# Block-local attention and two expert layers: how the first layer's weights are re-joined and split again, and when later weights are converted

## The chip, the cores and the metric

The kernel runs on one core of one Trainium2 chip. The metric is the device time of one execution in microseconds (us). Engines are named as in the profile: PE is TensorE (matrix products; PEld its weight loads), DVE is VectorE, ACT is ScalarE, POOL is GpSimd and SP is SyncE, which here only issues transfers. ACT also issues some transfers.

## The reference, cut to what matters

Everything is float32 in the inputs (the weights arrive as 64-bit floats, which the kernel converts from their integer halves).

```python
# attention: 4 x 8 heads, 768 positions of 64, in chunks of 32 with a short context
scores = scale * np.matmul(q_c, k_full.transpose(0, 1, 3, 2))
a = np.exp(scores - np.max(scores, axis=-1, keepdims=True))
out = np.matmul(a / (np.sum(a, axis=-1, keepdims=True) + 1e-09), v_full)
x = out.transpose(0, 2, 1, 3).reshape(3072, 512)
# first layer, 512 -> 1536 -> 512
x = (1.0 / (1.0 + np.exp(-(x @ w_gate))) * (x @ w_val)) @ w_out
# second layer, 512 -> 1024 -> 512
h = x @ w_in
solu = h * softmax(h)
ln = (solu - mean) / np.sqrt(var + 1e-06) * g_ln
return ln @ w_out2
```

## The kernel before, in words

**Blocks and stages.** The 3072 tokens are 24 tiles of 128, in 6 blocks of 512 (`j` from 0 to 5). Attention makes one tile of x at a time. For each block the up projection (`up`, line 694) goes over 12 chunks `m` of 128 hidden units, each for the gate and for the value: `up(j, m, gv)` is 12 matmuls of 128x512. Its result goes through a sigmoid (ACT, line 700) and a product (DVE, line 707 or 709) and is stored to DRAM. Only when all six blocks are up does the down projection start (line 801), followed by the second layer. TensorE runs the six blocks' up steps one after another, with the attention of later tiles between them.

**Two forms of the first layer's weights.** All products keep nearly float32 exactness by writing each operand as a high part plus a low part and adding three products. For blocks 0 and 1 the parts of a weight chunk are two 32-bit tiles, `wa[m]` (line 285 high, on ACT; line 236 low, on POOL). For blocks 2 to 5 they are two 16-bit tiles, `wh[m]`, which take the place of `wa[m]` in memory once `up(1, m, 1)` has read it. The re-making goes in steps:

- `r_max` (line 300): the absolute maximum of each of the 24 high parts, on DVE; `r_top` takes the largest per partition, and `hop` spreads it over the partitions (below).
- `r_set` (line 305): from the maxima a power of two as scale, in three small DVE instructions.
- `r_sum(m)` (line 308): high plus low back into one float32 tile `w32[m % 2]`, on POOL (recorded at line 312). There are two such tiles, so chunk m+2 waits for the low part of chunk m.
- `r_hi(m, gv)`: `w32` times the scale, rounded to 16 bits, on ACT (recorded at line 482).
- `r_lo(m, gv)`: `w32` times the scale minus the high part, on DVE (recorded at line 238, tile `wh`).

**A maximum over partitions.** `across` (line 461) does it on DVE alone: a 32x32 block transpose, a maximum, three copies of one element to the first partition (line 466), a maximum of four, four copies of one row of 32 equal elements back to partitions 0, 32, 64, 96 (line 469), another transpose. It is used 14 times.

**Later weights.** The weights of the three later products (28 pieces of 128x512) are loaded as 64-bit floats, converted (ACT line 220; DVE lines 225, 226, 229), scaled and split like the others and stored to DRAM (lines 401, 404). Before that, eight pieces of the last weight are loaded once more for their maxima alone (`p_load`, `p_max`), and block 0's twelve products are read back for theirs (`g_again`, `g_max0`). All these use a ring of three buffers `r`.

**The order.** A planner (`Plan`, line 18) orders all work by hand-given durations, dependencies, buffers and due times; the program text of each engine is its result, and each engine runs its queue strictly in that order. A task may start at most `AHEAD` = 40 us before its due time in the planner's own clock. Due times run back from the up steps, which are due one after another:

```python
FIRST, RATE, LEAD, SLACK, EARLY, LATER = 30.0, 1.12, 30.0, 3.0, 140.0, 235.0
one("wst", n, SP, 0.1, c_store, ..., due=LATER + 11.0 * (n - NU))          # later weights, n - NU from 0 to 27
one("rmax", n, DVE, 0.69, ..., ["whi"], due=FIRST + 70 + 2.5 * n)
one("pmax", i, DVE, 0.75, p_max, ["pld"], ..., due=EARLY + 8.0 * i)
add(("gmax", 0, m), DVE, 0.75, ..., due=EARLY + 4 + 8.0 * m)
```

`SHIFTS` adds small random shifts to the due times given by hand, from fixed seeds. Attention's loads of q, k and v, the stores of products, the transposes of x (line 672) and the reloads of block 0's products are issued on SP's queue; the later weights' loads and the eight loads for maxima on ACT's.

Of the kernel before, what the change touches and what calls it, by code (L numbers as in the profile page):

```python
# [9 lines left out]
F32 = mybir.dt.float32  # L10
# [11 lines left out]
class Plan:  # L22
# [7 lines left out]

    SHIFTS = [(2019, 0.3), (2226, 0.3), (6910, 1), (6082, 0.3), (4955, 0.3), (915, 0.3), (2444, 0.3)]

# [100 lines left out]
def encoder_kernel(  # L133
# [15 lines left out]
    nc = tc.nc  # L149
# [19 lines left out]
    const = ctx.enter_context(tc.tile_pool(name="const", bufs=1))  # L169
    turn = const.tile([128, 2, 32], F32, name="turn")  # L170
    tiny = const.tile([128, 4 * MF + 4 * K2 + 7 * NB + 22], F32, name="tiny")
# [119 lines left out]

    wh = {}

    def pow2_scale(s, p, m):
# [4 lines left out]
    def r_max(m, gv):  # L299
        absmax(WM[:, m, gv:gv + 1], wa[m][:, gv, 0].bitcast(F32))  # L300

    def r_top(gv):
        nc.vector.tensor_reduce(out=PG[:, gv:gv + 1], in_=WM[:, :, gv], axis=AX.X, op=ALU.max)

    def r_set():
        pow2_scale(SG, PG, PG)

# [10 lines left out]

    def r_lo(m, gv):
        lo_part(wh[m][:, gv, 1], W["f32"][:, m % 2, gv], wh[m][:, gv, 0], SG[:, gv:gv + 1])  # L320

# [5 lines left out]
    def absmax(dst, a):  # L327
        nc.vector.tensor_reduce(out=dst, in_=a, axis=AX.X, op=ALU.max, apply_absolute_value=True)  # L328
# [132 lines left out]
    def across(a):  # L461
        nc.vector.tensor_copy(turn[:, 0, 0:1], a)
        nc.vector.transpose(turn[:, 1], turn[:, 0])
        nc.vector.tensor_reduce(out=turn[:, 0, 1:2], in_=turn[:, 1], axis=AX.X, op=ALU.max)
        for x in range(1, 4):
            nc.vector.tensor_copy(turn[0:1, 0, 1 + x:2 + x], turn[32 * x:32 * x + 1, 0, 1:2])
        nc.vector.tensor_reduce(out=turn[0:1, 0, 5:6], in_=turn[0:1, 0, 1:5], axis=AX.X, op=ALU.max)
        for x in range(4):
            nc.vector.tensor_copy(turn[32 * x:32 * x + 1, 1], turn[0:1, 0, 5:6].to_broadcast([1, 32]))
        nc.vector.transpose(turn[:, 0], turn[:, 1])  # L470
        nc.vector.tensor_copy(a, turn[:, 0, 0:1])

    def hop(name, a, deps):
        add(name, DVE, 1.0, lambda: across(a), deps=deps + ["turn"])

# [489 lines left out]
    ACT, DVE, POOL, PE, SP = "act", "dve", "pool", "pe", "sp"  # L965
    FIRST, RATE, LEAD, SLACK, EARLY, LATER = 30.0, 1.12, 30.0, 3.0, 140.0, 235.0

# [22 lines left out]
    for t in range(NTILE):  # L990
# [23 lines left out]
        if t >= 4 * J16:  # L1014
            j = t // 4
            if t % 4 == 0:
# [5 lines left out]
                add(("isc", j), DVE, 0.2, lambda j=j: scales(j), deps=[("vset", j), "rset"])  # L1022
            one("xhi", t, ACT, 0.71, x_hi, ["norm", ("vset", j)], acq=[("w", ("xs", t))])
            one("xlo", t, DVE, 0.75, x_lo, ["xhi"], rel=[("s", t)])
            for y in range(2):
# [13 lines left out]
    for n, (m, gv, _) in enumerate(pieces):  # L1039
# [5 lines left out]
        if n >= NU:  # L1045
# [11 lines left out]
            if keep:  # L1057
                one("wlo", n, DVE, 0.76, c_lo, ["whi"], rel=[("w", n)])
            one("wst", n, SP, 0.1, c_store, ["wlo" if keep else ("w2imax", w2_piece.index(n))], rel=[key if keep else ("w", n)], dma=[0.73],
                due=LATER + 11.0 * (n - NU))  # L1060
            continue
# [3 lines left out]
        one("wlo", n, POOL, 1.4, w_lo, ["whi"], rel=[("w", n)])  # L1065
        one("rmax", n, DVE, 0.69, lambda n: r_max(*divmod(n, 2)), ["whi"], due=FIRST + 70 + 2.5 * n)
        if gv == 0:
            continue
        one("rsum", m, POOL, 2.5, r_sum, [("wlo", n - 1), ("wlo", n)] + [("rlo", m - 2, y) for y in range(2) if m > 1]
            + [("dx", 4 * J16 - 4)] * (m == 0),  # L1070
            acq=[("x", "w32")] if m == 0 else [])
        for z in range(2):
            add(("rhi", m, z), ACT, 0.72, lambda m=m, z=z: r_hi(m, z), deps=["rset", ("rsum", m), ("up", J16 - 1, m, 1, (0, 512))] + [("rhi", m, 0)] * z)
            add(("rlo", m, z), DVE, 0.76, lambda m=m, z=z: r_lo(m, z), deps=[("rhi", m, z)],
                rel=[("x", "w32")] if (m, z) == (MF - 1, 1) else [])
    for f in range(MF):
# [26 lines left out]
    for y in range(2):  # L1103
        add(("rtop", y), DVE, 0.1, lambda y=y: r_top(y), deps=[("rmax", 2 * m + y) for m in range(MF)])
        hop(("rspr", y), PG[:, y:y + 1], [("rtop", y)])
    add("rset", DVE, 0.3, r_set, deps=[("rspr", 0), ("rspr", 1)])
    clock = FIRST
    for j in range(NB):
        steps = steps_of(j)
        seen = set()  # L1110
        for s, (m, w) in enumerate(steps):
# [6 lines left out]
            for gv in range(2):  # L1118
                clock += (2.73 if j < J16 else 2.6) * RATE
                deps = [("up", j, m, 0, w)]  # L1120
                if gv == 0:
                    deps = [("wlo", 2 * m + x) if j < J16 else ("rlo", m, x) for x in range(2)] + [
                        ("xlo", 4 * j + x) if j < J16 else ("xtr", 4 * j + x, 1) for x in range(w[0] // 128, w[1] // 128)
                    ]
                elif s == len(steps) - 1:
                    deps += [("up", j, y, 1, z) for y, z in steps[:-1]]
                add(("up", j, m, gv, w), PE, 2.73 if j < J16 else 2.6, lambda j=j, m=m, gv=gv, w=w: up(j, m, gv, w),
                    deps=deps, acq=[] if gv else [("u0", key), ("u1", key)], due=clock,
                    rel=[("x", (y, j)) for y in "hl"[:2 if j < J16 else 1]] if gv and s == len(steps) - 1 else [])
# [154 lines left out]
```

## Time and profile before

| what | value |
|---|---|
| runs | 951.31 us median of 3 (949.44 to 952.26) |
| the profiled execution | 952.16 us, of which 950.4 us from the first to the last instruction (the span) |
| mean granted TensorE clock over the span | 0.983 |
| busy share of the span | PE 95%, PEld 51%, DVE 71%, ACT 51%, POOL 12% |
| blocks 0 to 5 start on TensorE at | 43.0, 136.2, 220.5, 307.1, 384.9, 461.3 us; the last up step ends at 523.6 |

A busy share is an average over stages with different limits. TensorE's matmuls are pipelined and their ends are modelled, so their busy time says that TensorE had work, not that it ran at its peak. The clock is given as a share of full speed (2.4 GHz). A row of a timeline carries in brackets how long its engine had been idle before it and what ended the wait; where that engine runs its queue in order, the wait's cause can lie further back.

### The profile page before, as it was taken

Reading aid. Unit: us, or ns where it says so; the run is one execution under the profiler, and the core shown is the slowest. Engines: PE = TensorE matmul, PEld = TensorE weight load, DVE = VectorE, ACT = ScalarE, POOL = GpSimd, SP = SyncE. Lnnn points to the kernel's source line nnn. Section 1 sums busy time; section 2 is a strip of 40 time slices with the busy share of each in tenths; the row PEclk is TensorE's granted clock in tenths of the full one; section 3 lists DMA queues with packets and bytes.
Section 4 is the critical chain, followed back from the end, with each engine's and each line's share of the span. In section 5 each row is a group of like instructions: output and inputs, shape, how many; then the busy total and the mean of one; then the engine's idle time right before and its main releaser. Section 6 shows DMA issues by size and latency. Waiting matters only on the chain.

```text
span 950.4 us, 18091 instructions
## 1 busy us (share of the span) xinstructions
PE 902.0 (95%) x7080; PEld 487.2 (51%) x7080; DVE 677.1 (71%) x1333; ACT 481.2 (51%) x810; POOL 117.6 (12%) x150
## 2 busy tenths in 40 slices
PE   5698998997899899999999999999999999999998
PEld 4486787774554454444444444444444444444443
DVE  3788999979874875788729556884874963867581
ACT  4467632733762692575546345553643633645452
POOL 1153330323200000000005200000000000000000
PEclk9699999999999999999999999999999999999999
DMA  9999946593797679655772622444154244242333
GB/s 171 272 215 242 219 114 179 135 215 98 188 197 164 205 164 194 195 146 145 257 272 100 213 89 75 92 100 99 56 119 97 73 101 100 67 100 45 78 67 99
DMA packets 219157, 136.85 MB, mean 144 GB/s; under 512 B 170176, under 2 KB 184512, under 8 KB 219072
## 3 DMA queue, kind: packets, MB, share of 16 engines
q1 hardware_dynamic: 208832, 109.48, 48.9%
q10 hardware_dynamic: 10240, 26.22, 9.1%
q8 instruction: 55, 0.90, 0.4%
q14 instruction: 30, 0.25, 0.1%
HBM read 86.38 MB, written 33.03 MB: 126 GB/s over the span
## 4 chain that ended last, share of the span: by engine, by line
PE 70%; DVE 15%; DMA 7%; issue 3%; ACT 2%; SPq 2%; POOL 0%; ACTq 0%; DVEq 0%; POOLq 0%
PE u L694 22%; PE y L801 19%; PE ps L944 13%; PE Q L854 5%; PE R L854 3%; PE P L854 3%; PE tr L496 3%; DVE tiny L328 2%; PE ps L555 2%; DVE w L226 2%; DMA r<-in_moe_w_in_dram 2%; DVE wh L238 1%; DVE w L225 1%; DVE g L709 1%; DMA mm<-in_mem_k_dram 1%
## 5 line engine op out<-in xcount | busy, mean ns | idle before, releaser
L694 PE MATMUL u<-x,wh 128*128 128x512 f16 x1152 | 255.4, 380 | 2.9 <-DMA x<-w 1.9
L694 PEld LDWEIGHTS <-wh 128*128 128x128 f16 x1152 | 112.1, 98 | 134.3 <-issue 5.6
L801 PE MATMUL y<-gh,pl 128*128 128x512 f16 x576 | 176.5, 379 | 1.1 <-ACT gh L482 1.1
L801 PEld LDWEIGHTS <-pl 128*128 128x128 f16 x864 | 84.5, 98 | 104.5 <-issue 2.9
L694 PE MATMUL u<-xh,wa 128*128 128x512 f32 x384 | 127.6, 404 | 3.8 <-DVE g L707 2.2
L944 PE MATMUL ps<-wo,nt 128*128 128x512 f16 x576 | 127.6, 379 | 0.8 <-ACT o L951 0.8
L482 ACT ACTIVATE gh<-gi,gm 128x512 f16<-128x512 f32 x72 | 51.3, 719 | 122.8 <-PE y L801 117.6
L801 PE MATMUL y<-gl,pl 128*128 128x512 f16 x288 | 109.1, 379 | 0.9 <-DVE gl L238 0.9
L238 DVE SCALAR_TENSOR_TENSOR gl<-gi,gm,gh 128x512 f16<-128x512 f32 x72 | 53.5, 749 | 62.6 <-ACT gh L482 62.4
L944 PEld LDWEIGHTS <-nt 128*128 128x128 f16 x576 | 56.3, 98 | 69.0 <-issue 1.1
L694 PEld LDWEIGHTS u<-xh,wa 128*128 128x128 f32 x384 | 73.8, 192 | 21.5 <-DVE g L707 3.3
L694 PE MATMUL u<-xl,wa 128*128 128x512 f32 x192 | 76.4, 398 | 0.4 <-DVE xl L680 0.4
L716 ACT ACTIVATE sg<-g,tiny 128x512 f32<-128x512 f32 x48 | 34.7, 722 | 55.6 <-DVE g L709 51.4
L709 DVE SCALAR_TENSOR_TENSOR g<-u,tiny,sg 128x512 f32<-128x512 f32 x48 | 35.8, 747 | 35.0 <-PE u L694 27.1
L854 PEld LDWEIGHTS <-yh 128*128 128x128 f16 x336 | 32.9, 98 | 39.6
L913 POOL TENSOR_TENSOR ls<-ls,tiny 128x1 f32<-128x1 f32 x24 | 14.8, 617 | 301.5 <-DVE ls L909 294.7
L220 ACT ACTIVATE w<-r 128x512 f32<-128x512 f32 x46 | 31.1, 676 | 35.6 <-DMA r<-in_moe_w_gate_dram 10.2
L875 DVE TENSOR_TENSOR pl<-Q,pl 128x512 f32<-128x512 f32 x36 | 24.7, 687 | 29.5 <-PE Q L854 29.4
L854 PE MATMUL Q<-pl,yh 128*128 128x512 f16 x144 | 42.8, 379 | 0.0
L700 ACT ACTIVATE sg<-u,tiny 128x512 f32<-128x512 f32 x48 | 32.8, 682 | 18.8 <-PE u L694 15.0
L694 PEld LDWEIGHTS u<-xl,wa 128*128 128x128 f32 x192 | 37.0, 193 | 8.1 <-DVE xl L680 0.9
L236 POOL TENSOR_TENSOR wa<-w,wa 128x512 fp32r<-128x512 f32 x24 | 33.2, 1386 | 60.0 <-ACT wa L285 60.0
(144 smaller groups left out, 1355.2 us busy)
## 6 DMA issues: line engine op xcount, KB each, us to landing
gd<-g SPq DMA_DIRECT2D x72, 256.0 KB
gi<-gd SPq DMA_DIRECT2D x72, 256.0 KB
r<-in_moe_w_out_dram ACTq DMA_DIRECT2D x28, 512.0 KB
vw<-in_v_dram SPq DMA_DIRECT2D x64, 98.0 KB
rk<-in_k_dram SPq DMA_DIRECT2D x24, 256.0 KB
rq<-in_q_dram SPq DMA_DIRECT2D x24, 256.0 KB
out_dram<-o SPq DMA_DIRECT2D x24, 256.0 KB
wd<-r SPq DMA_DIRECT2D x20, 256.0 KB
```

Source lines behind the costliest of these rows:

```text
L220: nc.scalar.activation(out=dst, in_=raw[:, :, 1].bitcast(F32), func=AF.Copy, scale=2.0 ** -112)
L236: nc.gpsimd.tensor_tensor(out=dst, in0=x, in1=hi, op=ALU.subtract)
L238: nc.vector.scalar_tensor_tensor(out=dst, in0=x, scalar=s, in1=hi, op0=ALU.mult, op1=ALU.subtract)
L482: nc.scalar.activation(out=dst, in_=x, func=AF.Copy, scale=s)
L496: nc.tensor.transpose(pv[:, kk, :], src[:, 2 * kk:2 * kk + 2, :], ident[0:rows, 0:rows])
L694: nc.tensor.matmul(u, lhsT=a, rhs=c[:, kk, w[0]:w[1]], start=(n == 0), stop=(n == 3 * KM - 1))
L700: nc.scalar.activation(out=sg, in_=U.pop((j, m, 0, w)), func=AF.Sigmoid, scale=1.0 if j < J16 else IS[:, j, 0:1])
L709: nc.vector.scalar_tensor_tensor(out=g, in0=u, scalar=IS[:, j, 1:2], in1=sg, op0=ALU.mult, op1=ALU.mult)
L716: nc.scalar.activation(out=rest, in_=g, func=AF.Square, scale=CS[:, j:j + 1], accum_out=GM[:, j, m:m + 1])
L801: nc.tensor.matmul(y, lhsT=a, rhs=c, start=(f == 0 and n == 0), stop=(f == MF - 1 and n == 2))
L854: nc.tensor.matmul(ps, lhsT=yc[a][:, c, kk, u * 128:(u + 1) * 128], rhs=t[:, hl, kk, :], start=(first and n == 0), stop=(n == 5), skip_gro ...
L944: nc.tensor.matmul(ps, lhsT=nt[:, a, kk, :], rhs=C["wo2"][:, c, kk, :], start=(n == 0), stop=(n == 3 * K2 - 1))
```

## The change

- The weight maxima become sums of squares on ACT, with the accumulator read that the product maxima of blocks 2 to 5 already use; two POOL powers (`r_root`) turn the largest sum into a scale.
- The joined weight `w32` is scaled by ACT in place (`r_scale`), which no longer waits for block 1's last use of the chunk; one ACT instruction per chunk rounds both halves to 16 bits (`r_hi2`), one POOL instruction subtracts for the low part (`r_lo2`).
- `across` copies one element to three partitions and fills the rows with one addition over 128x32.
- The maxima of the last weight and of block 0's products are due 95 us later; the later weights' stores are due from 275 us in steps of 10 instead of from 235 in steps of 11. A few planner durations and the seeds are new, and the x parts of tiles 8 and later wait for the last first-pass low part.

```diff
-    SHIFTS = [(2019, 0.3), (2226, 0.3), (6910, 1), (6082, 0.3), (4955, 0.3), (915, 0.3), (2444, 0.3)]
+    SHIFTS = [(203, 0.5), (476, 0.5), (6692, 0.3), (7115, 3), (2438, 0.3), (525, 0.5), (5342, 0.3)]
...
+    junk = stg[0].tile([128, 512], BF16, name="junk", bufs=1)
...
     def r_max(m, gv):
-        absmax(WM[:, m, gv:gv + 1], wa[m][:, gv, 0].bitcast(F32))
+        nc.scalar.activation(out=junk, in_=wa[m][:, gv, 0].bitcast(F32), func=AF.Square, scale=2.0 ** -16, accum_out=WM[:, m, gv:gv + 1])
 
     def r_top(gv):
-        nc.vector.tensor_reduce(out=PG[:, gv:gv + 1], in_=WM[:, :, gv], axis=AX.X, op=ALU.max)
+        a = PG[:, gv:gv + 1]
+        nc.vector.tensor_reduce(out=a, in_=WM[:, :, gv], axis=AX.X, op=ALU.max)
+        nc.vector.tensor_single_scalar(out=a, in_=a, scalar=2.0 ** -100, op=ALU.max)
+
+    def r_root():
+        for y in range(2):
+            nc.gpsimd.tensor_tensor(out=SG[:, y:y + 1], in0=PG[:, y:y + 1], in1=mhalf, op=ALU.pow)
 
     def r_set():
-        pow2_scale(SG, PG, PG)
+        nc.vector.tensor_single_scalar(out=SG, in_=SG, scalar=2.0 ** -2, op=ALU.mult)
+        pow2(SG)
+        nc.vector.reciprocal(out=PG, in_=SG)
...
-    def r_lo(m, gv):
-        lo_part(wh[m][:, gv, 1], W["f32"][:, m % 2, gv], wh[m][:, gv, 0], SG[:, gv:gv + 1])
+    def r_scale(m, gv):
+        hi_part(W["f32"][:, m % 2, gv], W["f32"][:, m % 2, gv], SG[:, gv:gv + 1])
+
+    def r_hi2(m):
+        wh[m] = wpool.tile([128, 2, 2, 512], F16, tag=f"wa{m}", name=f"wh{m}")
+        nc.scalar.copy(wh[m][:, :, 0], W["f32"][:, m % 2])
+
+    def r_lo2(m):
+        nc.gpsimd.tensor_tensor(out=wh[m][:, :, 1], in0=W["f32"][:, m % 2], in1=wh[m][:, :, 0], op=ALU.subtract)
...
-        for x in range(4):
-            nc.vector.tensor_copy(turn[32 * x:32 * x + 1, 1], turn[0:1, 0, 5:6].to_broadcast([1, 32]))
+        for x in range(1, 4):
+            nc.vector.tensor_copy(turn[32 * x:32 * x + 1, 0, 5:6], turn[0:1, 0, 5:6])
+        nc.vector.tensor_scalar(out=turn[:, 1], in0=turn[:, 2], scalar1=turn[:, 0, 5:6], scalar2=None, op0=ALU.add)
...
-        add(name, DVE, 1.0, lambda: across(a), deps=deps + ["turn"])
+        add(name, DVE, 2.0, lambda: across(a), deps=deps + ["turn"])
...
-    FIRST, RATE, LEAD, SLACK, EARLY, LATER = 30.0, 1.12, 30.0, 3.0, 140.0, 235.0
+    FIRST, RATE, LEAD, SLACK, EARLY, LATER = 30.0, 1.12, 30.0, 3.0, 235.0, 275.0
...
-            one("xhi", t, ACT, 0.71, x_hi, ["norm", ("vset", j)], acq=[("w", ("xs", t))])
-            one("xlo", t, DVE, 0.75, x_lo, ["xhi"], rel=[("s", t)])
+            one("xhi", t, ACT, 0.71, x_hi, ["norm", ("vset", j)] + [("wlo", 2 * MF - 1)] * (t > 7), acq=[("w", ("xs", t))])
+            one("xlo", t, DVE, 0.9, x_lo, ["xhi"], rel=[("s", t)])
...
-                due=LATER + 11.0 * (n - NU))
+                due=LATER + 10.0 * (n - NU))
...
-        one("rmax", n, DVE, 0.69, lambda n: r_max(*divmod(n, 2)), ["whi"], due=FIRST + 70 + 2.5 * n)
+        one("rmax", n, ACT, 0.95, lambda n: r_max(*divmod(n, 2)), ["whi"], due=FIRST + 90 + 2.5 * n)
...
         for z in range(2):
-            add(("rhi", m, z), ACT, 0.72, lambda m=m, z=z: r_hi(m, z), deps=["rset", ("rsum", m), ("up", J16 - 1, m, 1, (0, 512))] + [("rhi", m, 0)] * z)
-            add(("rlo", m, z), DVE, 0.76, lambda m=m, z=z: r_lo(m, z), deps=[("rhi", m, z)],
-                rel=[("x", "w32")] if (m, z) == (MF - 1, 1) else [])
+            add(("rsc", m, z), ACT, 0.72, lambda m=m, z=z: r_scale(m, z), deps=["rset", ("rsum", m)] + [("rsc", m, 0)] * z)
+        add(("rhi", m), ACT, 1.04, lambda m=m: r_hi2(m), deps=[("rsc", m, 1), ("up", J16 - 1, m, 1, (0, 512))])
+        add(("rlo", m), POOL, 2.45, lambda m=m: r_lo2(m), deps=[("rhi", m)], rel=[("x", "w32")] if m == MF - 1 else [])
...
-    add("rset", DVE, 0.3, r_set, deps=[("rspr", 0), ("rspr", 1)])
+    add("rroot", POOL, 1.3, r_root, deps=[("rspr", 0), ("rspr", 1), "mhalf"])
+    add("rset", DVE, 0.45, r_set, deps=["rroot"])
```

## Rows read from the trace of the kernel before

**Rows 1.** TensorE's blocks 0, 1, 2, 5: busy by engine (count), clock, DMA share, GB/s

```profile
43.00:136.20 93.20, 87.61 (x941) 70.45 (x942) 83.46 (x136) 56.56 (x104) 36.40 (x41) 0.96 0.94 215
136.20:220.50 84.30, 79.41 (x774) 62.82 (x773) 76.59 (x138) 36.39 (x59) 23.17 (x15) 0.98 0.71 167
220.50:307.10 86.60, 78.11 (x856) 40.06 (x857) 62.69 (x138) 44.68 (x89) 12.52 (x21) 0.98 0.69 153
...
461.30:523.60 62.30, 62.30 (x290) 28.24 (x289) 38.69 (x59) 33.81 (x54) 14.39 (x6) 1.00 0.59 205
```

**Rows 2.** timeline of TensorE, long waits of 156 to 238 us (start, length, [idle before])

```profile
156.14 0.66 PE L496 MATMUL tr<-ident,s 128*128 128x128 f32 x4 [2.39 <-ACT qT L544]
...
206.02 0.50 PE L694 MATMUL u<-xh,wa 128*128 128x512 f32 x1 [1.46 <-DVE g L707]
...
222.78 7.71 PE L694 MATMUL u<-x,wh 128*128 128x512 f16 x35 [1.94 <-DMA x<-w]
...
231.97 0.66 PE L496 MATMUL tr<-ident,rk 128*128 128x128 f32 x4 [1.48 <-ACT sg L700]
...
237.79 0.66 PE L496 MATMUL tr<-ident,rq 128*128 128x128 f32 x4 [2.58 <-DVE g L709]
```

**Rows 3.** timelines of ScalarE and GpSimd, what stood before those waits

```profile
155.50 0.59 ACT L544 COPY qT<-tr 128x512 f32<-128x512 f32 x1 [4.93 <-DVE tiny L328]
...
227.62 2.35 POOL L312 TENSOR_TENSOR w<-wa 128x1024 f32<-128x1024 f32 x1 [8.63 <-DVE tiny L341]
...
230.01 1.33 ACT L482 ACTIVATE wh<-w,tiny 128x512 f16<-128x512 f32 x2 [9.16 <-POOL w L312]
```

**Rows 4.** stretches of 5 us, granted clock behind the engines' busy times

```profile
155.00:160.00 5.00, 3.86 (x13) 3.13 (x14) 4.74 (x18) 2.00 (x6) 0.67 (x4) 0.72 0.84 229
240.00:245.00 5.00, 4.05 (x14) 1.45 (x12) 4.55 (x22) 1.78 (x5) 2.13 (x4) 0.75 0.80 176
```

**Rows 5.** groups of instructions, whole run: busy us, mean ns | idle before

```profile
L716 ACT ACTIVATE sg<-g,tiny 128x512 f32<-128x512 f32 x48 | 34.7, 722 | 55.6 <-DVE g L709 51.4 <-DMA wo<-wd 4.1
...
L312 POOL TENSOR_TENSOR w<-wa 128x1024 f32<-128x1024 f32 x12 | 29.2, 2439 | 68.4 <-DVE wh L238 47.2 <-PE u L694 8.7 <-DVE tiny L341 8.6
...
L238 DVE SCALAR_TENSOR_TENSOR wh<-w,tiny,wh 128x512 f16<-128x512 f32 x24 | 22.0, 943 | 0.0
...
L443 POOL TENSOR_TENSOR pl<-pl,pl 128x1024 f16<-128x1024 f32 x7 | 17.6, 2537 | 104.0 <-ACT pl L440 100.9 <-DVE w L229 3.1
...
L328 DVE TENSOR_REDUCE tiny<-wa 128x1 f32<-128x512 f32 x24 | 15.1, 674 | 0.0
...
L469 DVE COPY turn<-turn 1x32 f32<-1x32 f32 x56 | 14.3, 256 | 1.0
...
L716 ACT ACTIVATION_READ_ACCUMULATOR sg<-g,tiny 128x1 f32 x48 | 9.1, 190 | 0.0
...
L440 ACT CAST pl<-pl 128x1024 f16<-128x1024 f32 x7 | 7.1, 1034 | 0.4 <-PE u L694 0.4
...
L466 DVE COPY turn<-turn 1x1 f32<-1x1 f32 x42 | 6.0, 143 | 0.9
...
L732 POOL TENSOR_TENSOR tiny<-tiny 128x1 f32<-128x1 f32 x4 | 3.5, 864 | 82.1 <-DVE tiny L1163 82.1
```

**Rows 6.** one tile; one line (136 to 164 us): ns min/median/max, first and last start

```profile
L238 DVE SCALAR_TENSOR_TENSOR wh<-w,tiny,wh x24: 740/742/2872, 166.9 to 247.8; 128x512 f16<-128x512 f32 x24
...
L469 DVE COPY turn<-turn x12: 169/172/2339, 136.5 to 162.7; 1x32 f32<-1x32 f32 x12
```

**Rows 7.** chain that ended last: start us, length, instructions

```profile
440.59 67.46 PE u L694 x312
```

**Rows 8.** stretches where the transfers leave and where they go, columns as above

```profile
140.00:180.00 40.00, 37.60 (x411) 29.92 (x410) 38.74 (x91) 17.13 (x27) 6.73 (x7) 0.96 0.59 164
240.00:340.00 100.00, 95.89 (x1133) 50.14 (x1132) 72.55 (x167) 61.24 (x121) 8.30 (x25) 0.99 0.79 190
```

**Rows 9.** groups of VectorE instructions from 260 to 307 us

```profile
L328 DVE TENSOR_REDUCE tiny<-vw 128x1 f32<-128x2048 f32 x2 | 4.6, 2286 | 11.1 <-DMA vw<-mv 11.1
```

More of the change, by code (lines that the diff above doesn't have):

```diff
@@ L169, in encoder_kernel @@
     const = ctx.enter_context(tc.tile_pool(name="const", bufs=1))
-    turn = const.tile([128, 2, 32], F32, name="turn")
+    turn = const.tile([128, 3, 32], F32, name="turn")
     tiny = const.tile([128, 4 * MF + 4 * K2 + 7 * NB + 22], F32, name="tiny")
@@ L1065, in encoder_kernel @@
         one("wlo", n, POOL, 1.4, w_lo, ["whi"], rel=[("w", n)])
-        one("rmax", n, DVE, 0.69, lambda n: r_max(*divmod(n, 2)), ["whi"], due=FIRST + 70 + 2.5 * n)
+        one("rmax", n, ACT, 0.95, lambda n: r_max(*divmod(n, 2)), ["whi"], due=FIRST + 90 + 2.5 * n)
         if gv == 0:
             continue
-        one("rsum", m, POOL, 2.5, r_sum, [("wlo", n - 1), ("wlo", n)] + [("rlo", m - 2, y) for y in range(2) if m > 1]
+        one("rsum", m, POOL, 2.5, r_sum, [("wlo", n - 1), ("wlo", n)] + [("rlo", m - 2)] * (m > 1)
             + [("dx", 4 * J16 - 4)] * (m == 0),
@@ L1121, in encoder_kernel @@
                 if gv == 0:
-                    deps = [("wlo", 2 * m + x) if j < J16 else ("rlo", m, x) for x in range(2)] + [
+                    deps = [("wlo", 2 * m + x) if j < J16 else ("rlo", m) for x in range(2)] + [
                         ("xlo", 4 * j + x) if j < J16 else ("xtr", 4 * j + x, 1) for x in range(w[0] // 128, w[1] // 128)
```

## Prediction, made before the change was run

> **What bounds the kernel now.** I read the stretches first: one call that cuts the span where TensorE starts token block 0, 1, 2 and so on. The reader is to see that TensorE is busy for 79.4 of block 1's 84.3 us and 78.1 of block 2's 86.6 us, so it is idle for 4.9 and 8.5 us, 13.4 together; in block 5 it never waits [rows 1]. VectorE is busy for 76.6 of the 84.3 us of block 1, and 83.5 of 93.2 in block 0 [rows 1]. TensorE is the limit everywhere else; in blocks 1 and 2 it waits for something that VectorE's queue holds back.
>
> Then the timeline of TensorE, for its long waits: 2.39 us at 156, 1.46 at 206, 1.94 at 222.8, 1.48 at 232.0 and 2.58 at 237.8, together 9.85 us [rows 2]. Two name VectorE's product, one a transposed x that VectorE's part precedes, two ScalarE. So I ask what held ScalarE and GpSimd. In their timelines ScalarE idled 4.93 us behind a VectorE maximum before the qT copy at 155.5, and GpSimd 8.63 us behind VectorE's work on the last weight's maxima (line 341) before the weight sum at 227.6; ScalarE's low-precision weights then waited 9.16 us for that sum [rows 3]. All five waits lead back to VectorE.
>
> Last, the granted clock. After the long waits it averages 0.72 over 155 to 160 us and 0.75 over 240 to 245 [rows 4], so it is partly at 1.2 GHz, the lower of its two levels; at 2.4 GHz that time holds 0.28 and 0.25 times 5 us more work, 2.65 us. What blocks 1 and 2 can give back is therefore 13.4 + 2.65 = **16.0 us**.
>
> **The change part by part.**
>
> Weight maxima. 24 VectorE maxima of 0.674 us go, 15.1 us on its engine [rows 5]. ScalarE gets 24 squares with an accumulator read. The squares of the product maxima are that form: 0.722 + 0.190 = 0.912 us [rows 5], 21.9 us in all. ScalarE is busy for 36.4 of 84.3 us in block 1 but 56.6 of 93.2 in block 0 [rows 1], and some squares can go there. Bound on TensorE: from 0 (they fill ScalarE's idle time) to 5.6 us, which would double block 0's idle time of 93.2 - 87.6; I take 1, because the due times (120 us and later in the planner) lie mostly past block 0's crowded first half. The root is two GpSimd powers of 0.864 us [rows 5], 1.7 us more in a chain that ends with the scales near 164; the first low part comes at 166.9 [rows 6], and TensorE wants it only at 220, so this is hidden by block 1 and would show only if the chain were 50 us late.
>
> Joined weights. 24 VectorE low parts go, 22.0 us [rows 5]. ScalarE keeps its 24 scalings and gets 12 conversions of twice the length, 12 x 1.034 = 12.4 us; GpSimd gets 12 subtractions. The nearest GpSimd row is the same form (f16 from f32, 128x1024), 2.537 us, so 30.4 us beside its 12 sums of 2.439 [rows 5]. Per weight chunk GpSimd works 4.98 us. Run wholly in series (sum 2.44, two scalings at the square's 0.72, conversion 1.03, low part 2.54) a chunk takes 7.4 us, and 12 of them 89 us: from 164 to 253. TensorE uses one chunk per 5.19 us (67.46 us for 312 matmuls, 24 a chunk [rows 7]) plus attention, about 7.2 us in block 2 (86.6 / 12), so its last chunk is due near 300. The low parts before took from 166.9 to 247.8 [rows 6]. I take 0 for it; at the ends, -2 us (chunks ready sooner) and +5 (below).
>
> What GpSimd does to VectorE shows in the rows: a low part has a median of 0.742 us but a longest of 2.872, and a row copy a median of 0.172 but a longest of 2.339 [rows 6], about one GpSimd sum more. The means of all, 0.943 and 0.256 [rows 5], put the loss at 24 x 0.20 + 56 x 0.084 = 9.5 us over 12 sums, 0.8 us per long GpSimd instruction. Twelve more cost VectorE about 9.5 us by this.
>
> The Trainium skill, GPSIMD Engine Reference, Key points, says that GpSimd shares its SBUF interfaces with VectorE, which contends in instructions with two SBUF inputs or in a two-port mode, and that VectorE is about twice as fast at elementwise work. The trace agrees with both (2.54 us against two of 0.742), and by that rule alone this part would be a loss. What it would do here is rival (b).
>
> Row copies. 56 copies of 0.256 us become 42 copies of one element at 0.143 and 14 additions over 128x32, which I put at 0.256 for want of a row: 14.3 - 6.0 - 3.6 = 4.7 us less on VectorE [rows 5]. Only the chain before the scales and the block maxima see it; beyond VectorE's relief I take 0 (ends 0 and -2).
>
> Later conversions. Eight loads and maxima of w2_out and twelve reloads and maxima of block 0's products are due 95 us later, 20 x 0.674 = 13.5 us of VectorE out of block 1 (the shape of the weight maxima [rows 5]); the conversions start 40 us later and end 13 us later (275 + 270 against 235 + 297). What moves is 8 x 512 KB on ScalarE's DMA queue and 12 x 256 KB on SP's, 7.34 MB. Where they leave, the DMA engines are 0.59 busy; where they go (240 to 340) 0.79 at 190 GB/s [rows 8]. At 190 / 0.79 = 240 GB/s they need 31 us, against 21 us free; the conversions that leave this stretch (40 us at one piece of 0.77 MB per 11 us, 2.8 MB) give back 12. It just fits: I take 1 us, ends 0 and 18 (below). At the other end VectorE is busy for 38.7 of block 5's 62.3 us [rows 1], which covers one or two more pieces; if not, they meet the start of the down projection, 0 to 4 us; I take 1.
>
> The planner's durations, its new random shifts and the x order reorder every queue slightly: 0, ends -4 and +4. That later x parts wait for the last first-pass low part costs nothing: GpSimd had done it long before the first of them.
>
> **Sum.** VectorE loses 15.1 + 13.5 + 22.0 + 4.7 = 55.3 us and is held 9.5 longer: some 46 us of relief, nearly all of it in blocks 1 and 2. It is then no longer the last to arrive, and the five waits (9.85 us) and the clock loss (2.65) go, 12.5 us; what remains of the 16.0 I leave standing. New costs 1 + 1 + 1 = 3. Net -9.5 on the profiled execution's 952.16 us gives 942.7; that execution was 0.85 above the median of the runs, so **942 us**.
>
> **Rivals.**
> (a) *Latency instead of VectorE.* The waits pass to the attention chain (ScalarE's copies, loads, transposes), and only 2 us or less is gained: about 950. For it: VectorE itself waited 11.1 us for v loads in block 2 [rows 9], so loads are the next to be late. Against it: all five waits lead back to VectorE. 0.10.
> (b) *GpSimd eats the relief.* VectorE is held by each of 24 long GpSimd instructions for a whole 2.5 us, not 0.8, 60 us, more than the 55 that the change takes from it; block 2's share of the gain, about 6 us with its clock, is lost: near 948. Against: the maxima, which have one input, are not stretched (mean 0.674 [rows 5]), and the row copies and low parts, which are, leave VectorE. 0.10.
> (c) *Slower: the moved loads starve block 3.* The 20 transfers lie ahead of block 3's v loads. In the 60 us before block 3 starts at 307, only 0.21 x 60 = 12.6 us of the DMA engines is free, so v comes 31 - 12.6 = 18 us late, and TensorE, in order, has nothing else: 942 + 18 = 960. SP's queue adds to it, since a reload that waits for one of three buffers holds the attention loads behind it. It decides from 9.5 us of delay on. Against: the pieces moved out, and due times that put attention first. 0.10.
> (d) The change does what it says (the forms are in the code); I give no chance to the opposite.
>
> **How the numbers follow.** Forecast 0.70, (a) 0.10, (b) 0.10, (c) 0.10. A measurement of this kernel can tell about 0.3%, 2.9 us, from no change: 948.5 to 954.2. The forecast's own range is 931 to 948: 16 us and 4 of reordering at one end, half the gain eaten by the upper bounds at the other. With (a) and most of (b) the range is 931 to 953; (c) is left out, and a little of the forecast's tail. Faster: 0.70 and half of (b), 0.75; same: (a) and most of the rest of (b), 0.14; slower: (c) and a remnant, 0.11.
>
> **What would show it.** Right: TensorE's idle time in blocks 1 and 2 falls from 13.4 us to about 4; VectorE's share of block 1 falls from 0.91 to about 0.6; the clock stays at 1.00 from 150 to 245; the low parts on GpSimd end before 255; the row copies have no 2 us outlier. Wrong: TensorE waiting for x from a transpose, or for v, at the start of block 2 or 3 with DMA above 0.9 (c); TensorE waiting for GpSimd's low parts, or VectorE's instructions stretched beside them (b); or waits as long as before under new names (a).

## The result and the profile after

| | before | after | predicted |
|---|---|---|---|
| median of the runs on one chip | 950.60 us (949.44 to 952.26) | **935.49 us** (933.94 to 937.92) | 942 (931 to 953) |
| ratio | | 0.9842, 95% interval 0.9813 to 0.9871 | |
| profiled execution, span | 952.16, 950.4 us | 936.47, 934.7 us | |

The kernel is faster by 15.1 us. The direction and the range held; the forecast from 951.31 to 942 was a gain of 9.3, so the measured gain is 5.8 us larger.

First the stretches again, cut where TensorE starts token block 0, 1, 2 and 3 of the changed kernel (columns as in [rows 1]; the last row is all that follows).

```profile
41.70:135.70 94.00, 89.95 (x1012) 72.14 (x1013) 78.95 (x135) 70.80 (x142) 36.08 (x41) 0.95 0.89 206
135.70:210.70 75.00, 75.00 (x708) 61.26 (x707) 46.69 (x110) 54.97 (x91) 53.72 (x34) 1.00 0.53 120
210.70:293.20 82.50, 76.18 (x857) 39.83 (x857) 44.15 (x91) 44.93 (x84) 7.80 (x17) 0.98 0.78 177
...
293.20:934.70 641.50, 632.28 (x3914) 294.15 (x3911) 444.91 (x913) 328.25 (x519) 39.97 (x51) 1.00 0.49 133
```

Block 1 is 75.0 us instead of 84.3, and TensorE is busy in all of it; it also holds 66 fewer matmul instructions, because the new order places attention's products elsewhere. Block 2 is 82.5 instead of 86.6, block 0 94.0 instead of 93.2 (with 71 more matmul instructions in it). VectorE's share of block 1 is 46.69 / 75.00 = 0.62 instead of 0.91. From block 0's start to block 3's the kernel takes 251.5 us instead of 264.1, with nearly equal work on TensorE (2577 instructions against 2571): its idle time in the three blocks went from 5.59 + 4.89 + 8.49 = 18.97 to 4.05 + 0 + 6.32 = 10.37 us, and its busy time from 245.13 to 241.13. Of these 4.0 us the granted clock explains 2.3 (busy time times the missing share of the clock, in stretches of 1 us: 7.2 before, 4.9 after); the rest is not explained. With a start 1.3 us earlier that is 13.9 of the span's 15.7 us. From block 3 on the same work takes 641.5 us instead of 643.3.

Next, TensorE's long waits. The five of [rows 2] are gone: between 136 and 286 us it never waits for more than 0.1 us. One new wait ends block 2 (timeline of TensorE, with the idle time before the instruction in brackets), and the granted clock falls with it (stretches of 5 us, columns as above):

```profile
292.34 1.11 PE L513 MATMUL tr<-ident,rq 128*128 128x128 f32 x4 [6.32 <-DVE tiny L296]
```

```profile
155.00:160.00 5.00, 5.00 (x88) 4.09 (x87) 1.61 (x3) 4.68 (x7) 3.17 (x2) 1.00 0.01 3
240.00:245.00 5.00, 5.00 (x86) 2.75 (x85) 4.53 (x10) 4.76 (x6) 0.00 (x0) 1.00 0.01 3
289.00:294.00 5.00, 1.66 (x6) 1.15 (x7) 4.50 (x21) 1.33 (x3) 0.00 (x0) 0.56 0.14 52
294.00:299.00 5.00, 5.00 (x19) 2.07 (x18) 4.11 (x9) 1.57 (x4) 0.00 (x0) 0.76 0.88 233
```

The first two answer to [rows 4], where the clock was 0.72 and 0.75; now it is full there. In the stretch with the end of the 6.32 us wait it is 0.56 and in the next 0.76, so TensorE spends part of block 3's beginning at 1.2 GHz although it has work.

What the new instructions cost (groups, columns as in [rows 5], and the low parts by their tile, as in [rows 6]):

```profile
L321 POOL TENSOR_TENSOR w<-wa 128x1024 f32<-128x1024 f32 x12 | 28.8, 2402 | 4.3 <-PE u L711 3.6
L336 POOL TENSOR_TENSOR wh<-w,wh 128x1024 f16<-128x1024 f32 x12 | 26.7, 2224 | 12.3 <-ACT wh L333 12.3
L301 ACT ACTIVATE junk<-wa 128x512 bf16<-128x512 f32 x24 | 15.1, 629 | 0.3
L333 ACT CAST wh<-w 128x1024 f16<-128x1024 f32 x12 | 12.5, 1046 | 0.3
L301 ACT ACTIVATION_READ_ACCUMULATOR junk<-wa 128x1 f32 x24 | 4.6, 191 | 0.0
L486 DVE TENSOR_SCALAR turn<-turn 128x32 f32<-128x32 f32 x14 | 4.5, 325 | 0.5
L310 POOL TENSOR_TENSOR tiny<-tiny 128x1 f32<-128x1 f32 x2 | 1.1, 555 | 5.9 <-DVE tiny L488 5.9
```

```profile
L336 POOL TENSOR_TENSOR wh<-w,wh x12: 2126/2152/2615, 156.8 to 215.2; 128x1024 f16<-128x1024 f32 x12
```

Most are near the predicted prices; the square (0.820 us with its read, against 0.912), the low part (2.22 against 2.54) and the power (0.555 against 0.864) are cheaper, the filling addition (0.325 against 0.256) dearer. The last low part starts at 215.2, before the 220 to 300 us in which TensorE wants them.

**Where the new wait comes from.** VectorE's timeline, with its queue in order, shows a maximum between two products (L726) of block 2; the chain of waits (start, length) shows what it waited for, and SyncE's timeline (SPq: issues) where its load stood:

```profile
277.59 0.74 DVE L726 SCALAR_TENSOR_TENSOR g<-u,tiny,sg 128x512 f32<-128x512 f32 x1
286.56 2.29 DVE L344 TENSOR_REDUCE tiny<-vw 128x1 f32<-128x2048 f32 x1 [8.24 <-DMA r<-gd]
...
291.42 0.15 DVE L488 COPY tiny<-turn 128x1 f32<-128x1 f32 x1
291.53 0.75 DVE L726 SCALAR_TENSOR_TENSOR g<-u,tiny,sg 128x512 f32<-128x512 f32 x1
```

```profile
274.61 6.83 DMA r<-in_moe_w_in_dram
282.63 3.92 DMA r<-gd
286.56 2.30 DVE tiny L344
```

```profile
277.83 1.22 SPq L689 DMA_TRANSPOSE x<-w  x1
281.51 0.36 SPq L765 DMA_DIRECT2D gd<-g  x1
281.91 0.67 SPq L639 DMA_DIRECT2D vw<-mv  x2
282.63 0.82 SPq L738 DMA_DIRECT2D r<-gd  x2
```

The maximum of block 4's v (2.29 us) comes after 8.24 us without work on VectorE. A 512 KB load of a later weight is under way from 274.61 to 281.44; the last pieces of v (vw) are issued only at 281.91, behind a transpose and a store of products, and a reload of block 0's products (r), moved here by the change, follows directly. The profile names the reload, the last to land, as what released the maximum; the maximum reads v, and in the kernel with the changed instructions alone (below) a like idle time of 4.49 us ends with v. Behind the maximum the hop over the partitions runs to 291.57, and only then comes the product; it ends at 292.28, just before TensorE starts again (the profile names the small instruction L296 behind it). This looks like the mechanism of rival (c), for block 4's v rather than block 3's. That the moved transfers cause it is not shown: the kernel with the changed instructions alone has them at their old times and still waits 4.87 us behind block 4's v, while the changed kernel with the old due times and the new seeds has no such wait.

### The profile page after: what moved, and what is told of

Read it like the earlier page. It is cut to its first block, busy times and chain, and to the rows that moved or that the text cites. A ratio compares the mean times of both kernels' runs of the same rounds, so it can differ in the third digit from the quotient of the medians.

```text
span 934.7 us, 18116 instructions
## 1 busy us (share of the span) xinstructions
PE 896.9 (96%) x7080; PEld 486.5 (52%) x7080; DVE 634.1 (68%) x1287; ACT 517.1 (55%) x876; POOL 143.7 (15%) x164
## 4 chain that ended last, share of the span: by engine, by line
PE 81%; DMA 6%; DVE 5%; issue 3%; ACT 2%; SPq 1%; ACTq 0%; POOL 0%; DVEq 0%; POOLq 0%
PE u L711 32%; PE y L818 18%; PE ps L961 13%; PE Q L871 5%; PE R L871 3%; PE P L871 3%; PE tr L513 3%; PE ps L572 3%; DMA vw<-mv 1%; DMA gd<-g 1%; DMA mm<-in_mem_k_dram 1%; DVE w L226 1%; DMA r<-in_moe_w_in_dram 1%; DMA vw<-in_v_dram 1%; DVE w L225 1%
## 5 line engine op out<-in xcount | busy, mean ns | idle before, releaser
L930 POOL TENSOR_TENSOR ls<-ls,tiny 128x1 f32<-128x1 f32 x24 | 16.1, 672 | 348.4 <-DVE ls L926 225.6
L726 DVE SCALAR_TENSOR_TENSOR g<-u,tiny,sg 128x512 f32<-128x512 f32 x48 | 35.8, 748 | 38.2 <-PE u L711 26.9
L344 DVE TENSOR_REDUCE tiny<-vw 128x1 f32<-128x2048 f32 x8 | 18.3, 2285 | 33.8 <-DMA vw<-mv 16.6
```

Source lines behind the costliest of these rows:

```text
L726: nc.vector.scalar_tensor_tensor(out=g, in0=u, scalar=IS[:, j, 1:2], in1=sg, op0=ALU.mult, op1=ALU.mult)
```

## The experiments

The theory on trial: VectorE's queue was late in blocks 1 and 2, and the work taken from it is the gain. The rivals: GpSimd gives it back; or not the instructions but the new order (due times and seeds) is what gained. Each kernel was timed beside the kernel before on one chip, in five rounds. The changed kernel, run once more, with the last two experiments:

> The changed kernel itself, unedited, as the yardstick for the two moves: 934 to 938 by the earlier runs; any theory that is right says the same here.

It took 935.71 us, ratio 0.9845 [0.9819, 0.9872], with a wait of 6.38 us at 290. Below, "the changed kernel" is this 0.9845.

### VectorE's work put back, in the same order

Only the maxima back on VectorE:

```diff
-        nc.scalar.activation(out=junk, in_=wa[m][:, gv, 0].bitcast(F32), func=AF.Square, ...)
+        absmax(WM[:, m, gv:gv + 1], wa[m][:, gv, 0].bitcast(F32))
...
+        nc.vector.tensor_scalar(out=a, in0=a, scalar1=a, scalar2=2.0 ** -32, op0=ALU.mult, op1=ALU.mult)
```

> The changed kernel, every queue in the same order, but the 24 weight maxima are taken by VectorE (0.674 us each, 16 us) where ScalarE took squares; the scale then comes from the largest square instead of the largest sum of squares. Theory (VectorE's load is what TensorE waits for): most of the 24 fall between 89 and 146 us, where VectorE is 0.84 busy in block 0 and 0.62 in block 1, so VectorE fills up in the end of block 0 and waits come back there: 2 to 5 us, 937.5 to 940.5. Rival 1 (the gain is the new order, not the load): within 1.5 us of the changed kernel's 935.5. Rival 2 (ScalarE's 22 us of squares cost block 0): faster, 931 to 934.

Only the low parts back, 12 of 128x1024:

```diff
-        nc.gpsimd.tensor_tensor(out=wh[m][:, :, 1], in0=W["f32"][:, m % 2], in1=wh[m][:, :, 0], op=ALU.subtract)
+        nc.vector.tensor_tensor(out=wh[m][:, :, 1], in0=W["f32"][:, m % 2], in1=wh[m][:, :, 0], op=ALU.subtract)
```

> The changed kernel, every queue in the same order, but the 12 low parts are subtracted by VectorE (some 1.08 us each, 13 us) at the same places where GpSimd did it. Theory: VectorE is busy for 46.7 of block 1's 75.0 us, so 13 us more still fit: 0 to 2.5 us slower, 935.5 to 938. Rival 1 (order): 934 to 937, no wait in blocks 1 and 2. Rival 2 (GpSimd's 12 long instructions hold VectorE up and cost time): faster by 1 to 3, 932.5 to 934.5, with fewer stretched VectorE instructions.

Both edits together:

> Both together: VectorE gets 29 us back between 89 and 215 us, in the same order. Theory: VectorE's busy share from 89 to 215 goes from about 0.7 to above 0.9 and waits of TensorE come back in blocks 0, 1 and 2: 5 to 10 us slower, 940 to 946, more than e1 and e2 added up. Rival 1 (order): 934 to 938.

Measured: the maxima 940.80 us, ratio 0.9900 [0.9875, 0.9924]; the low parts 938.45, 0.9871 [0.9845, 0.9897]; both 942.27, 0.9916 [0.9888, 0.9943]. Against the changed kernel's 0.9845 (a ratio from another set of runs) that is 5.2, 2.5 and 6.8 us of 951. The first and the third stand clear of it; the second is not told apart from nothing. (940.80 and 938.45 lie 0.3 and 0.45 us above the ranges expected.) Block 1 of the kernel with the maxima, of that with the low parts and of that with both (stretches, columns as above):

```profile
138.80:217.50 78.70, 75.65 (x706) 60.86 (x704) 59.11 (x133) 50.33 (x76) 53.32 (x34) 1.00 0.51 115
```

```profile
137.30:212.60 75.30, 75.05 (x708) 61.26 (x707) 54.95 (x119) 54.81 (x90) 28.96 (x22) 1.00 0.55 118
```

```profile
136.40:217.20 80.80, 77.05 (x706) 62.13 (x704) 63.05 (x139) 48.86 (x75) 29.17 (x23) 0.98 0.57 110
```

VectorE busy 46.7, 55.0, 59.1, 63.1 us gives TensorE 0, 0.25, 3.05 and 3.75 us of idle time in the block. With the maxima back the waits return under VectorE's name (timeline of TensorE in that block):

```profile
157.03 0.66 PE L514 MATMUL tr<-ident,s 128*128 128x128 f32 x4 [1.25 <-DVE g L725]
166.16 0.66 PE L514 MATMUL tr<-ident,s 128*128 128x128 f32 x4 [1.63 <-DVE g L725]
```

So in this order VectorE's load does set block 1's waits. In another order the same load need not: the kernel with the changed instructions alone (below) has VectorE busy for 66.0 us of its block 1, and TensorE is idle for 0.46 us there. That both together cost more than the sum of the two was not borne out (6.8 against 7.7). The Trainium skill, GPSIMD Engine Reference, Key points, calls VectorE about twice as fast at elementwise work; by that alone the low parts would do better on VectorE. The trace agrees for the single instruction: a low part of 128x1024 took 1.22 us (median) on VectorE in this run against 2.15 on GpSimd. The time of the kernel, if anything, went the other way: here it counts whose queue TensorE waits for.

### The row copies

```diff
-        for x in range(1, 4):
-            nc.vector.tensor_copy(turn[32 * x:32 * x + 1, 0, 5:6], turn[0:1, 0, 5:6])
-        nc.vector.tensor_scalar(out=turn[:, 1], in0=turn[:, 2], scalar1=turn[:, 0, 5:6], scalar2=None, op0=ALU.add)
+        for x in range(4):
+            nc.vector.tensor_copy(turn[32 * x:32 * x + 1, 1], turn[0:1, 0, 5:6].to_broadcast([1, 32]))
```

> The changed kernel, every queue in the same order, but the 14 maxima over partitions copy whole rows of 32 as before (4 copies of 0.17 us or more instead of three of one element and one addition over 128x32). Theory: 14 x 0.35 us more on VectorE, hidden: 935 to 937; one or two copies last above 2 us where a long GpSimd instruction runs beside them. Rival (the copies sit in the chain that sets the scale and the later block maxima, and a 2 us copy delays products behind it): 938 to 941.

935.97 us, 0.9852 [0.9825, 0.9878]: no difference that can be told, as the prediction had it. The longest row copy was 2.29 us.

### The order: due times and seeds

Two edits, each applied to either kernel. The old due times in the changed kernel are this diff, in the kernel before its reverse; the old or new seeds are the one line `SHIFTS` of the change.

```diff
-    FIRST, RATE, LEAD, SLACK, EARLY, LATER = 30.0, 1.12, 30.0, 3.0, 235.0, 275.0
+    FIRST, RATE, LEAD, SLACK, EARLY, LATER = 30.0, 1.12, 30.0, 3.0, 140.0, 235.0
...
-                due=LATER + 10.0 * (n - NU))
+                due=LATER + 11.0 * (n - NU))
```

The changed kernel with the old seeds:

> The changed kernel with the random shifts of the kernel before, so all queues are ordered anew. Theory (the relief of VectorE carries the gain, the seeds only shuffle): blocks 1 and 2 together stay below 162 us against 171 before and 157.6 after; total 933 to 942. Rival 1 (the seeds carry the gain): 945 to 951.

The kernel before with the new seeds:

> The kernel before with the changed kernel's random shifts alone. Theory: VectorE is as loaded as before, so 947 to 955, and VectorE above 0.85 busy in block 1. Rival 1 (the seeds carry the gain): 936 to 944.

The changed kernel with the old due times:

> The changed kernel with the old due times (maxima of the last weight and block 0's products from 140 us, later weights from 235 us in steps of 11). Theory: 13.5 us of VectorE come back into block 1, which has 28 us free, so blocks 1 and 2 lose 1 to 4 us; the 6.3 us wait at the end of block 2 behind block 4's v maximum may go, since the transfers leave that place: 934 to 941. Rival 3 (moving these transfers and maxima is what made the gain): 943 to 950.

The kernel before with the new due times:

> The kernel before with the new due times alone. Theory: VectorE loses 13.5 of 76.6 us in block 1 but keeps the weight maxima and the low parts: 943 to 949. Rival 3: 936 to 941.

The changed instructions (with their engines, planner durations and dependencies) under both the old due times and the old seeds:

> The changed kernel's instructions and dependencies with both the old due times and the old seeds, beside the changed kernel's 935.7 us and the kernel before's 951. If the gain is mostly the instructions (VectorE's relief, less the 13.5 us of moved maxima, which stay in block 1), the time is 940 to 945, blocks 1 and 2 together are 162 to 166 us against 170.9 before and 157.6 after, and some wait of 2 us or more for VectorE is left in block 1. If the parts of the order (due times worth 8 and seeds worth 3.6 in the changed kernel) simply add up, it is about 947. If the order carries the gain, it is within 3 us of the kernel before, 948 to 954.

| instructions | due times | seeds | median us | ratio to before | blocks 1, 2 us |
|---|---|---|---|---|---|
| before | old | old | 951 | 1 | 84.3, 86.6 |
| before | old | new | 957.69 | 1.0072 [1.0046, 1.0098] | 84.8, 86.1 |
| before | new | old | 963.08 | 1.0127 [1.0109, 1.0144] | 87.7, 82.0 |
| changed | old | old | 948.76 | 0.9979 [0.9958, 0.9999] | 80.6, 91.0 |
| changed | old | new | 943.68 | 0.9926 [0.9907, 0.9945] | 84.9, 78.3 |
| changed | new | old | 939.29 | 0.9879 [0.9861, 0.9897] | 78.3, 81.1 |
| changed | new | new | 935.7 | 0.9845 [0.9819, 0.9872] | 74.8, 82.6 |

The parts do not add up. The new instructions alone give 2.7 us, the new due times alone cost 12, the new seeds alone 7, and all together gain 15. So the gain belongs neither to the instructions nor to the order by itself: the same instructions are worth 2.7 us under the old order, 14.0 with the new seeds (957.69 to 943.68) and 23.8 with the new due times (963.08 to 939.29). The kernel before with both was not run; nor were the two due times apart (the maxima's and the later weights'), nor the new planner durations and the x order, which here always go with the changed instructions. Of the expectations, that for the changed kernel with the old seeds held; the new seeds in the kernel before came 2.7 us above their range, the old due times in the changed kernel fell to rival 3, the new due times in the kernel before missed even the sign, and the changed instructions alone came out in their last case, that of the order. Lengths of one block compare loosely, since the orders place attention's matmuls differently (774 instructions in block 1 before, 914 with the changed instructions alone). Three timelines show what the queues did.

*New due times, old instructions.* TensorE's longest wait of block 1 and what VectorE did before it:

```profile
160.79 1.11 PE L496 MATMUL tr<-ident,s 128*128 128x128 f32 x4 [7.39 <-DVE g L707]
```

```profile
147.86 3.64 DVE L328 TENSOR_REDUCE tiny<-wa 128x1 f32<-128x512 f32 x6
...
152.92 0.15 DVE L462 COPY turn<-tiny 128x1 f32<-128x1 f32 x1
...
157.77 0.15 DVE L471 COPY tiny<-turn 128x1 f32<-128x1 f32 x1
...
160.05 0.68 DVE L707 TENSOR_TENSOR g<-sg,u 128x512 f32<-128x512 f32 x1
```

The moved maxima are out of block 1 (VectorE is busy 73.5 us there), but the planner draws the weight maxima together in their place: six of them at 147.86, and then, from 152.9, the two hops and the scales in one row ahead of the product of 160.05. So with less work on VectorE in the block, a longer run of it ahead of one product made a longer wait. Yet blocks 1 and 2 together are no slower than before (169.7 against 170.9 us); most of the loss lies in block 3, 85.4 us instead of 77.8. There TensorE waits for a transposed x (timeline of TensorE; stretch, columns as above; before, the DMA share was 0.58 in this stretch and TensorE had no wait):

```profile
310.51 11.63 PE L694 MATMUL u<-x,wh 128*128 128x512 f16 x47 [4.16 <-DMA x<-w]
```

```profile
305.00:311.00 6.00, 1.84 (x6) 0.38 (x5) 2.17 (x6) 2.20 (x5) 0.00 (x0) 0.78 0.95 193
```

This is the sign that the prediction gave for rival (c), near the start of block 3 and with DMA above 0.9: in the kernel before, the new due times alone bring it about.

*Old due times, new instructions and seeds.* The same place, with the squares gone from VectorE but the moved maxima back in its queue (r and gm); TensorE waited 3.51 us for the product of 162.40 (timelines of TensorE and of VectorE):

```profile
163.13 1.11 PE L513 MATMUL tr<-ident,s 128*128 128x128 f32 x4 [3.51 <-DVE g L724]
```

```profile
157.94 0.68 DVE L344 TENSOR_REDUCE gm<-r 128x1 f32<-128x512 f32 x1
...
160.32 2.15 DVE L238 SCALAR_TENSOR_TENSOR w<-s,tiny,w 128x512 f16<-128x512 f32 x1 [1.10 <-ACT w L499]
162.40 0.68 DVE L724 TENSOR_TENSOR g<-sg,u 128x512 f32<-128x512 f32 x1
```

The maxima are not all of it: the part of x just before the product took 2.15 us, with a GpSimd low part beside it from 159.80 to 161.92, against a median of 0.75.

*Changed instructions alone.* Block 1 gains 3.7 us; block 2 loses 4.4, and TensorE's idle time goes from 4.89 to 0.46 us in the one and from 8.49 to 13.26 in the other. From block 0's start to block 3's this kernel takes 264.5 us, against 264.1 before; what it gains lies behind. Block 2's stretch, TensorE's waits in it, and the conversions of later weights that lie on VectorE in it (one of the three instructions per piece: ns min/median/max, first and last start):

```profile
216.20:307.20 91.00, 77.74 (x782) 38.46 (x782) 66.83 (x133) 45.92 (x90) 14.91 (x20) 0.94 0.69 161
```

```profile
225.51 5.34 PE L711 MATMUL u<-x,wh 128*128 128x512 f16 x24 [1.40 <-DVE g L724]
...
237.01 4.22 PE L711 MATMUL u<-x,wh 128*128 128x512 f16 x12 [3.21 <-DVE g L726]
...
297.45 7.73 PE L711 MATMUL u<-x,wh 128*128 128x512 f16 x26 [4.87 <-DVE tiny L296]
```

```profile
L226 DVE SCALAR_TENSOR_TENSOR w<-r,w x10: 691/693/2501, 218.1 to 307.1; 128x512 int32<-128x512 int32 x10
```

The kernel before has 4 such instructions in block 2, the changed kernel 2, this one 10. VectorE's busy time in blocks 1 and 2 sums to 132.9 us, against 139.3 before and 90.8 in the changed kernel. So much of the room that the change made was filled: a task may start 40 us before it is due, the conversions were due from 235 us, and with VectorE free the planner pulled them into block 2, where each piece takes some 3.2 us of VectorE (a low part, three conversion steps and a maximum):

```profile
226.09 0.74 DVE L238 SCALAR_TENSOR_TENSOR r<-w,tiny,r 128x512 f16<-128x512 f32 x1
226.75 0.42 DVE L225 TENSOR_SCALAR w<-w 128x512 int32<-128x512 int32 x1
227.20 0.70 DVE L226 SCALAR_TENSOR_TENSOR w<-r,w 128x512 int32<-128x512 int32 x1
227.94 0.69 DVE L229 SCALAR_TENSOR_TENSOR w<-r,w 128x512 int32<-128x512 int32 x1
228.66 0.69 DVE L344 TENSOR_REDUCE tiny<-w 128x1 f32<-128x512 f32 x1
```

In the first two waits above they stand ahead of the product that TensorE waits for (224.76, 236.20). They were also stretched there, which is rival (b)'s mechanism: in front of the first, two conversion steps took 2.50 and 2.72 us, each with a GpSimd instruction beside it, instead of 0.69 (the first of them below); in front of the second, an operation on 128x2 took 2.10 (last section).

```profile
218.08 2.50 DVE L226 SCALAR_TENSOR_TENSOR w<-r,w 128x512 int32<-128x512 int32 x1
```

The third wait is not theirs but that of block 4's v. The later due times keep the conversions out, and the moved maxima with them; the two together are worth 9.5 us with the old seeds (948.8 to 939.3) and 8.0 with the new. How much of it is the conversions' was not measured.

### The new wait taken away

The maximum of block 4's v and its hop are issued after the second next product instead of before it:

```diff
-    for part in plan.order():
+    todo = plan.order()
...
+    put_after({("vmax", 9), ("vtop", 4), ("vspr", 4), ("vset", 4)}, ("mul", 2, 11, (0, 512)))
+    for part in todo:
         part["fn"]()
```

> The changed kernel with one move on VectorE's queue: the maximum of block 4's v (which waited 8.24 us for its loads with two products of block 2 behind it) and the three steps after it are issued behind the product of chunk 11 of block 2; all else in the same order. Theory: TensorE's wait of 6.32 us at 286 goes, and the clock loss after it (0.02 of block 3's 76 us, 1.5 us): 6 to 8 us faster, 927.5 to 930. Rival (TensorE meets the next late thing, x of block 3 or 4 from the same loads): 932 to 936, with a wait of 3 us or more between 286 and 310 or at the start of block 4.

And with block 4's first product moved forward as well:

```diff
+    put_after({("mul", 4, 0, (0, 512))}, ("up", 4, 0, 1, (0, 512)))
```

> The same move, and the product of chunk 0 of block 4 is issued on VectorE as soon as its matmuls are, ahead of the conversions of two later weights that stood before it (TensorE waited 2.22 us for it at 383). Theory: 1.5 to 2.5 us faster than with the first move alone, 925.5 to 928. Rival: the conversions come later and their stores, so the wait moves to the down projection's start: same as with one move.

The first took 936.34 us, 0.9837 [0.9814, 0.9860]: no gain, a miss (6 to 8 us were expected; its rival had 932 to 936 with a wait of 3 us or more, and the waits are shorter). Block 2 did shrink to 77.3 us, but blocks 2 to 4 together are 234.4 us, against 234.6 in the changed kernel beside it. TensorE's waits after block 2:

```profile
289.02 0.39 PE L711 MATMUL u<-x,wh 128*128 128x512 f16 x1 [1.49 <-DMA x<-w]
...
312.17 0.66 PE L513 MATMUL tr<-ident,rq 128*128 128x128 f32 x4 [1.46 <-DVE g L726]
...
381.21 0.65 PE L513 MATMUL tr<-ident,rq 128*128 128x128 f32 x4 [2.21 <-DVE g L726]
```

TensorE arrives earlier at block 3 and waits there for transposed x, and then for products; the clock is 0.978 in blocks 3 and 4, against 0.987 and 1.00. Over blocks 2 to 4 TensorE is idle for 6.8 us instead of 9.1, but busy for 227.5 instead of 225.6. The wait was in large part slack taken at one place instead of several. The second move makes 933.39 us, 0.9805 [0.9781, 0.9830], 3.0 below the first, where 1.5 to 2.5 were expected; blocks 2 to 4 are 231.5 us there. It is the fastest kernel here, but its interval still overlaps the changed kernel's.

## Why the prediction was right, and where it was not

**What bounds the kernel: right in the main.** With VectorE at 0.62 of block 1 the five waits are gone and the clock is full from 150 to 245. VectorE's work put back in the same order brings waits back in block 1, longer the more is put back. That all five waits led back to VectorE is too strong. For the 1.94 us on a transposed x, VectorE's last part of x was done at 207.34, and the next transpose was issued at 213.74 after SyncE's queue had waited 4.7 us for a load of a later weight. And GpSimd's sum of 227.6 waited, by the code, for the low parts that ended at 227.46, not for line 341; those too are VectorE's.

**What the change does to VectorE: right in the sum, wrong in what was enough.** The step that failed is "the planner's durations, its new random shifts and the x order reorder every queue slightly: 0, ends -4 and +4", and with it the costing of the later due times by transfers and the 13.5 us of maxima alone. The changed instructions under the old order gave 2.7 us; the new order on top of them gave the other 13, 8.0 to 9.5 of it by the due times and 3.6 to 5.1 by the seeds, while without them the same due times and seeds cost 12 and 7. In the new order the maxima and low parts off VectorE are worth 6.8 us. The relief came as forecast, with VectorE's busy time in blocks 1 and 2 down from 139.3 to 90.8 us, but it paid only with the order. The seeds' share is luck as far as the forecast goes: with the old seeds the time is 939.3, nearer to 942. I counted relief and did not ask what the planner would put into it, although the rule (40 us ahead of due) and the due times stood in the code.

**The sum.** Measured on the span to block 3's start, the gain is 8.6 us of idle time, 4.0 of TensorE's busy time (2.3 by the clock) and 1.3 at the start. Term by term: what I left standing in blocks 1 and 2 (13.4 - 9.85 us of short waits) went as well. The squares in block 0, put at +1, cost no idle time there that can be told (5.59 to 4.05 us; 5.76 in the second profiled execution of the changed kernel). The late conversions at the start of the down projection, put at +1, did not show: from block 3 on the kernel gains 1.8. The moved transfers, put at +1, can have a part in the wait of 6.32 us and the clock after it, which is not shown. Its removal gave nothing, so it cannot be counted as a loss of that size.

**Costed at nothing.** The chain of scale and low parts was done by 218 us, well ahead of 253; the power pair took 1.1 us instead of 1.7; the row copies gave nothing.

**The rivals.** (a) did not happen. (b): the stretched instructions are real. The sum took 9.5 us more of them; in the changed kernel they are fewer. Counting by how much VectorE's instructions exceed the lower quartile of their group while a GpSimd instruction runs (those by over 0.15 us), from 130 to 256 us, 15.0 us before became 5.5, although GpSimd's long instructions doubled. That is mostly the order: with the changed instructions alone it is still 11.2 us, and some of TensorE's waits in block 2 end behind such instructions. (c) did not come in the changed kernel at block 3; its sign came in the kernel before with the new due times.

**What would show it.** Idle time in blocks 1 and 2: 6.32 us, in one wait, instead of about 4. VectorE's share of block 1: 0.62, as forecast. Clock full from 150 to 245: so it was. Low parts done before 255: so they were. No 2 us outlier in the row fill: the longest addition is 1.40 us.

## What to carry to other kernels

Work taken off the engine that is late paid little here while the scheduler refilled the gap with work that could wait: look at what may start early, and move its due time with the relief. An order made for one set of instructions says little about another: test both in both before crediting either. The wait removed late in this chain of just-in-time stages mostly moved on to the next stage, so price such a wait by what arrives second.

## What the runs showed of the hardware

Small instructions on VectorE can last as long as a GpSimd instruction beside them. In the kernel with the changed instructions alone, an operation on 128x2 elements, 0.22 us elsewhere, took 2.10 us in one of four and ended within 0.02 us of GpSimd's low part (timelines of GpSimd and of VectorE):

```profile
233.72 2.12 POOL L336 TENSOR_TENSOR wh<-w,wh 128x1024 f16<-128x1024 f32 x1 [3.09 <-issue]
```

```profile
233.76 2.10 DVE L653 TENSOR_SCALAR tiny<-tiny 128x2 f32<-128x2 f32 x1
```

Maxima of one 128x512 input did not stretch: none of them is above 0.69 us before or in the changed kernel, among them the 12 that lie wholly within a GpSimd instruction of over 2 us. The number of inputs alone does not tell the forms apart, since the row copies, which have one input too, did stretch [rows 6]. The square with accumulator took 0.629 us here against 0.722 for the product's squares [rows 5], and the low part 2.22 us against 2.54 for the same form there.
